# A rehearsal of the final store: the same small store, issued once behind the last weight loads

## The chip, the cores and the metric

One core of one Trainium2 chip. The metric is the device time of one execution in microseconds. The executions of one kernel lie within about 0.5 us of each other here (0.04% of the time). That is larger than the effect studied. So the verdicts below rest on durations inside the traces, which repeat to about 0.02 us. The times are given beside them. The experiments ran on three chips.

Short names used throughout: PE is TensorE, DVE is VectorE, ACT is ScalarE, SP is SyncE. SP issues 78 of the 80 DMAs of the kernel before, ACT the other two.

## The reference, cut to what matters

The whole is a decode step: attention of 2 batch rows over a cache of 32 heads x 16384 positions, mixed by a gate with a small MLP.

```python
x = A_x                                   # (2, 1, 1024) bf16
g = sigmoid((x * gate_w).sum(-1, keepdims=True))
a = attention(x, k_cache, v_cache, wq) @ wo   # caches: 2 x 32 x 16384 x 128 bf16
b = mlp_block(x, w1, w2, w3, w4)
return g * a + (1 - g) * b                # (2, 1, 1024) bf16: 4 KB
```

Two facts matter. The caches and weights are 572 MB to be read once. The output is 4 KB.

## The kernel before: the parts that the change and the argument touch

All work is recorded by a helper, so most instructions have the helper's line, L82. `lane` is the semaphore that the helper has a DMA raise by 16 (`then_inc(lane[0], 16)`), with the value that others wait for; `waits` are further waits. If an operation has several waits, all but the last become wait instructions of their own ahead of it, and the last is carried by the operation itself:

```python
waits = [self.target(o) for o in self.plan[id(op)]] + op.waits
for sem, value in waits[:-1]:
    eng.wait_ge(sem, value)
ins = op.emit()
for sem, value in waits[-1:]:
    ins._wait_ge(sem, value)
```

The start (two small loads on ACT's queue), the end of the loads, and the final store:

```python
R.scalar.dma_start(out=x_rows[0:B, :], in_=A_x..., lane=(row_in[0], 16))
R.scalar.dma_start(out=x_rows[B : B + 1, :], in_=gate_w..., lane=(row_in[1], 16))
# ... weights, 32 K and 32 V loads of the caches on SP, all compute ...
w4 = load_pieces(next_slot(), 0, B_w4, W4_SPLIT, ...)          # 2 pieces
wo = load_pieces(next_slot(), 0, A_wo, WO_SPLIT, ...)          # 7 pieces
R.meet()
# ... the loops over the cache ...
st_down(w4)
wo_stage(wo)
rows = t_tile([P, QW], BF16)
R.vector.tensor_copy(out=rows, in_=out_acc)                     # the cast
R.sync.dma_start(
    out=out.rearrange("b s (g n) -> g (b s) n", g=NQ),          # 4 x 2 rows of 512 B
    in_=rows[0 : P : APART, :],                                 # 8 partitions
    lane=(row_in[0], 32),
)
# ...
nc.sync.wait_ge(row_in[0], 32)
```

`h_rows`, which the change uses as a source, is a tile of the MLP that is written once, at 43.8 us, and read by nobody.

## Time and profile before

| | before |
|---|---|
| time, median of 3 runs | 1329.58 us (1329.5 to 1329.78) |
| span of the profiled execution | 1327.8 us |
| DMA | 572.70 MB, mean 431 GB/s |
| final store: issue on SP / issue to last landing | 0.696 us / 1.740 us |
| end of the cast to SP passing the store's completion ("the stretch") | 1.784 us |

The page of the kernel before: the span, the busy time and share of each engine, and the DMA engines' busy share in 40 equal slices of the span, in tenths.

```profile
span 1327.8 us, 11371 instructions
...
PE 801.6 (60%) x4806; PEld 305.4 (23%) x4859; DVE 762.7 (57%) x1009; ACT 27.2 (2%) x68; POOL 13.2 (1%) x41
...
DMA  9999999999999999999999999999999999999998
```

No compute engine is busy for more than 60% of the span, and the DMA engines are busy at nine tenths or more in every slice but the last. The kernel is bound by its loads until the last byte of weights has landed. What the change can shorten is what follows that moment.

The chain of waits that ended last, over the last 50 us of the kernel before (start, length, what):

```profile
1279.52 44.26 DMA slot<-in_A_wo_dram
1323.78 0.04 issue
1323.83 0.42 PE out_acc L82 x3
1324.24 0.02 issue
1324.27 0.42 DVE T L82
```

The timeline of the tail of the kernel before (start, length, engine, operation), the issues of SP included:

```profile
1276.41 11.12 SPq L82 DMA_DIRECT2D slot<-in_A_wo_dram  x7
...
1323.83 0.39 PE L82 MATMUL out_acc<-slot,T 128*17 128x256 bf16 x4 [0.23 <-DMA slot<-in_A_wo_dram]
1324.27 0.42 DVE L82 CAST T<-out_acc 128x256 bf16<-128x256 f32 x1 [16.30 <-PE out_acc L82]
1324.72 0.70 SPq L82 DMA_DIRECT2D out_dram<-T  x1
```

And of SP's own waits, the one for that store:

```profile
SPq L1027 <- DMA out_dram<-T: 1.0, 1, 1.0
```

Read together: the last piece of `A_wo` lands at 1323.78, four matmuls and the cast take until 1324.69, SP issues the store for 0.70 us and then waits 1.0 us for it to land. About 1.27 us of closing barriers follow. So 4 us of 1327.8 lie behind the loads, and the store is 1.76 us of them.

### The profile page before, as it was taken

Reading aid. Unit: us, or ns where it says so; the run is one execution under the profiler, and the core shown is the slowest. Engines: PE = TensorE matmul, PEld = TensorE weight load, DVE = VectorE, ACT = ScalarE, POOL = GpSimd, SP = SyncE. Lnnn points to the kernel's source line nnn. Section 1 sums busy time; section 2 is a strip of 40 time slices with the busy share of each in tenths; the row PEclk is TensorE's granted clock in tenths of the full one; section 3 lists DMA queues with packets and bytes.
Section 4 is the critical chain, followed back from the end, with each engine's and each line's share of the span. In section 5 each row is a group of like instructions: output and inputs, shape, how many; then the busy total and the mean of one; then the engine's idle time right before and its main releaser. Section 6 shows DMA issues by size and latency. Waiting matters only on the chain. (4 is left out here: it accounts for less than half of the span.)

```text
span 1327.8 us, 11371 instructions
## 1 busy us (share of the span) xinstructions
PE 801.6 (60%) x4806; PEld 305.4 (23%) x4859; DVE 762.7 (57%) x1009; ACT 27.2 (2%) x68; POOL 13.2 (1%) x41
## 2 busy tenths in 40 slices
PE   2767766555566655555765555576655557665553
PEld 1212222122222222222221222222222222222222
DVE  2277676655557665555666555566655556665540
ACT  0000000000000000000000000000000000000000
POOL 0000000000000000000000000000000000000000
PEclk9698887777888877778887777888777788877776
DMA  9999999999999999999999999999999999999998
GB/s 406 443 431 429 433 439 432 434 428 442 432 434 428 442 430 436 428 442 426 438 430 441 426 440 430 440 426 436 434 440 426 436 434 440 426 436 434 440 419 357
DMA packets 11118, 572.70 MB, mean 431 GB/s; under 512 B 1239, under 2 KB 1247, under 8 KB 1634
## 3 DMA queue, kind: packets, MB, share of 16 engines
q1 hardware_dynamic: 11100, 572.53, 99.6%
q8 instruction: 8, 0.13, 0.0%
q14 instruction: 4, 0.03, 0.0%
q10 hardware_dynamic: 6, 0.01, 0.0%
HBM read 572.53 MB, written 0.00 MB: 431 GB/s over the span
## 5 line engine op out<-in xcount | busy, mean ns | idle before, releaser
L526 PE MATMUL S<-T,z 128*128 128x512 bf16 x1933 | 571.6, 426 | 310.7 <-DVE T L517 298.8
L517 DVE STREAM_TRANSPOSE T<-slot 128x1024 f32<-128x1024 f32 x496 | 593.2, 1229 | 247.6 <-DVEq L921 196.0
L526 PEld LDWEIGHTS S<-T,z 128*128 128x128 bf16 x1984 | 171.1, 104 | 698.0 <-DVE T L517 532.5
L577 PE MATMUL O<-slot,PT 128*32 128x512 bf16 x2048 | 119.6, 387 | 7.2 <-PEq L921 7.2
L577 PEld LDWEIGHTS O<-slot,PT 128*32 128x32 bf16 x2048 | 74.0, 140 | 52.2 <-issue 23.0
L588 DVE TENSOR_SCALAR mix<-O,xmask 128x128 f32<-128x128 f32 x32 | 11.2, 351 | 103.6 <-PE O L577 103.6
L543 PE MATMUL tot<-rs,ones_f 128*128 128x2 f32 x62 | 18.2, 363 | 76.4 <-DVE rs L568 76.4
L560 ACT ACTIVATE mix<-S,nb 128x512 bf16<-128x512 f32 x31 | 21.3, 687 | 1158.3 <-DVE nb L550 1158.3
L596 PE MATMUL oc<-asel,mix 128*128 128x2 f32 x64 | 12.3, 262 | 51.8 <-DVE mix L591 51.8
L535 DVE TENSOR_REDUCE m<-S 128x1 f32<-128x512 f32 x31 | 21.4, 691 | 36.3 <-PE S L526 36.3
L565 DVE STREAM_TRANSPOSE PT<-mix 128x512 bf16<-128x512 bf16 x31 | 22.0, 711 | 26.2 <-ACT mix L560 26.2
L591 DVE SCALAR_TENSOR_TENSOR mix<-O,xmask,mix 128x128 f32<-128x128 f32 x96 | 33.7, 351 | 3.4
L543 PEld LDWEIGHTS tot<-rs,ones_f 128*128 128x128 f32 x62 | 15.5, 311 | 82.3 <-DVE rs L568 82.3
L543 PE MATMUL mall<-mix,ones_f 128*128 128x128 f32 x62 | 15.1, 326 | 16.3 <-DVE mix L538 16.3
L596 PEld LDWEIGHTS oc<-asel,mix 128*128 128x128 f32 x64 | 9.5, 188 | 66.2 <-DVE mix L591 66.2
L547 DVE TENSOR_REDUCE mx<-mall 64x1 f32<-64x64 f32 x62 | 13.8, 222 | 18.4 <-PE mall L543 18.0
L82 PE MATMUL out_acc<-slot,T 128*17 128x256 bf16 x240 | 12.1, 361 | 17.1 <-DMA slot<-in_A_wo_dram 9.3
L508 POOL TENSOR_TENSOR z<-qsel,own 128x32 bf16<-128x32 bf16 x31 | 10.5, 340 | 1167.3 <-PE O L577 1167.3
L82 PE MATMUL S<-T,z 128*128 128x512 bf16 x62 | 17.9, 416 | 6.3 <-DVE T L82 5.9
L82 DVE STREAM_TRANSPOSE T<-slot 128x1024 f32<-128x1024 f32 x16 | 19.1, 1228 | 1.6 <-PE S L82 1.3
L573 DVE RECIPROCAL rinv<-tot 128x2 f32<-128x2 f32 x31 | 5.3, 170 | 21.1 <-PE tot L543 21.1
L599 DVE TENSOR_TENSOR OT<-oc,rinv 128x2 f32 x32 | 5.1, 159 | 15.2 <-PE oc L596 15.2
(115 smaller groups left out, 129.5 us busy)
## 6 DMA issues: line engine op xcount, KB each, us to landing
slot<-in_B_w_dram SPq DMA_DIRECT2D x1, 7168.0 KB, 48.5
slot<-in_B_w_dram SPq DMA_DIRECT2D x2, 3584.0 KB, 28.4
slot<-in_A_wo_dram SPq DMA_DIRECT2D x3, 2048.0 KB, 37.2
slot<-in_B_w_dram SPq DMA_DIRECT2D x2, 2048.0 KB, 29.2
slot<-in_A_wo_dram SPq DMA_DIRECT2D x1, 1024.0 KB, 43.5
slot<-in_A_k_cache_dram SPq DMA_DIRECT2D x32, 49.3
slot<-in_A_v_cache_dram SPq DMA_DIRECT2D x32, 35.1
slot<-in_A_wo_dram SPq DMA_DIRECT2D x1, 512.0 KB, 44.3
```

The costliest lines, as they stand in the source:

```text
L82: op = Op(engine, lambda: getattr(eng, method)(*args, **kwargs), reads, writes, waits, lane)
L517: return vector.transpose(out=t_tile([P, 2, CJ, 32], FP32, m % 2).rearrange("p w j s -> p j w s"), in_=K[:].bitcast(FP32)[:, m * CW : (m + ...
L526: return tensor.matmul(S, lhsT=z[:, v, NM - 1 - m : NM - 1 - m + P], rhs=Tb[:, v // 2, :, v % 2], start=(m == 0 and v == 0), stop=(m == NM ...
L535: return vector.reduce_max(out=stat["m"][:], in_=S, axis=AX.X)
L543: return tensor.matmul(ps, lhsT=ones_f[:], rhs=src, start=True, stop=True)
L547: return vector.reduce_max(out=stat["mx"][pa, :], in_=mall[pa, pa], axis=AX.X)
L560: return scalar.activation(out=Pr, in_=S, func=ACTF.Exp, bias=stat["nb"][:], scale=scale, accum_out=stat["rs"][:])
L565: return vector.transpose(out=PT[:], in_=Pr)
L577: return tensor.matmul(O[32 * g : 32 * g + 32, :], lhsT=PT[:, m : CJ * 32 : 16], rhs=V[:].rearrange("p (j d) -> p j d", d=Dh)[:, j0 : j0 + ...
L588: return vector.tensor_scalar(out=Os, in0=Ox, scalar1=xmask[:, 0:1], scalar2=None, op0=ALU.mult)
L591: return vector.scalar_tensor_tensor(out=Os, in0=Ox, scalar=xmask[:, x : x + 1], in1=Os, op0=ALU.mult, op1=ALU.add)
L596: return tensor.matmul(oc, lhsT=Os, rhs=asel[:], start=True, stop=True)
```

## The change: its intent, and the diff

The idea is to pay in advance what the first store of this form may cost. A store of the same shape (the same rows of the output, 8 source partitions of 512 B; only the step between the source partitions differs, 8 in place of 16) is issued behind the last weight loads, while SP has nothing to do (in the kernel before, its last load issue ends at 1287.53 us and its next issue begins at 1324.72). The final store overwrites what it writes, so it must come second. The order of issue on SP alone can't be relied on for that: with a rehearsal of one row (below), the rehearsal landed at 1322.26 us and the piece of `A_wo` issued before it at 1323.77. So the final store now waits for the first one too. Without the wait, that would be a race.

```diff
         [(sem["free"], 2 * LAST + 2)],
     )
+    out_rows = out.rearrange("b s (g n) -> g (b s) n", g=NQ)
+    R.sync.dma_start(out=out_rows, in_=h_rows[0:64:8, 0:QW], lane=(row_in[1], 32))
     R.meet()
 ...
     R.sync.dma_start(
-        out=out.rearrange("b s (g n) -> g (b s) n", g=NQ),
-        in_=rows[0 : P : APART, :],
+        out=out_rows,
+        in_=rows[0:P:APART, :],
         lane=(row_in[0], 32),
+        waits=[(row_in[1], 32)],
     )
```

The final store now has two waits, so by the code shown above the wait for the cast becomes an instruction of its own, and the store carries the wait for the rehearsal.

## The prediction

> What bounds the kernel now. The page shows DMA busy at nine tenths or more in 39 of 40 slices and 431 GB/s over the span of 1327.8 us (572.53 MB read): the load queue is the limit, PE (60%) and DVE (57%) are not. The change touches only the tail, read from the timeline of the last 60 us, the chain of waits, and the trace's packet and semaphore records:
>
> - SP issues the seven pieces of A_wo from 1276.41. The seventh is held in the queue for 8.0 us (1279.52 to 1287.53) until the last V load has landed (1287.27).
> - The last 2 KB packets end at 1323.47, the last piece lands at 1323.78, PE finishes at 1324.24, the DVE cast runs 1324.27 to 1324.69.
> - The final store is issued at 1324.72; its issue takes 0.70 us on SP; its 512-byte packets run 1326.02 to 1326.12; SP passes its completion wait at 1326.48. Issue to landing is 1.76 us; 1.27 us of closing barriers follow.
>
> What the change adds. One more 4 KB store in the same queue, of rows that are overwritten (8 packets of 512 B, some 25 ns each). SP should reach it at about 1287.6; as the seventh A_wo piece had to wait for an older load, I expect the new issue to be held too, until the first B_w4 piece lands (about 1295.7). SP is free until 1324.7, so this costs nothing. Its packets stand behind the last A_wo piece[...]. They should run by 1323.6 at the latest and land some 0.35 us later (as the final store's did), about 1323.9: 0.8 us before the final store is ready. The new wait should be met. The second wait costs the final store one more sequencer instruction, 0.04 to 0.08 us (gaps between SP's instructions in the tail).
>
> What it may save. The final store is the first of its form on SP. Its issue takes 696 ns, while A_wo and cache loads take 327 to 432. On the ACT queue the first small load took 542 ns and the second, of a slightly different form, 234 ns. If a first use of a form costs extra, a rehearsal some 30 us earlier removes 0.2 to 0.5 us of the 1.76 us, all on the critical path. But the form itself may cost it[...]: one early update at 1325.79, then four at 1326.40 to 1326.46. Such a cost stays. Estimate: save 0.35, pay 0.06, net -0.3 us.
>
> Predicted: 1329.3 us, 80% range 1328.7 to 1329.9. Faster by over 2%: 0.2%; within 2%: 99.6%; slower by over 2%: 0.2%.
>
> What would show it. Right: a second store of 4 KB in the table of issues; the last A_wo landing, PE and cast unmoved within 0.1 us; the final store's issue shorter than 0.70 us, and issue to landing 1.3 to 1.6 us. Wrong in the saving: its issue again near 0.70 us and landing again 1.76 us after; then the time is 1329.6 to 1329.7.
>
> What would make it wrong. The rehearsal lands later than 1324.7, so the final store waits for it: up to 1 us slower. Or another chip moves all by more than the effect.

The rehearsal delays no load (measured: the last load landed 0.05 us later, within the spread between runs).

## The result, and the profile after

The time is 1329.52 us (median of 6 runs, 1329.42 to 1329.69), against 1329.61 us for the kernel before in 6 runs (1329.36 to 1329.78). The ratio is 0.9999, with a 95% interval of 0.9987 to 1.0012. A ratio is the mean time of one kernel's fast runs over that of the other's in the same rounds, so it is not quite the ratio of the medians quoted. By the times alone the two kernels are the same.

The same lines of the page after the change:

```profile
span 1327.7 us, 11373 instructions
...
PE 800.0 (60%) x4806; PEld 304.5 (23%) x4859; DVE 763.1 (57%) x1009; ACT 27.2 (2%) x68; POOL 13.1 (1%) x41
...
DMA  9999999999999999999999999999999999999998
```

The chain of waits after the change, over the same stretch:

```profile
1279.32 44.51 DMA slot<-in_A_wo_dram
1323.83 0.04 issue
1323.87 0.42 PE out_acc L82 x4
1324.29 0.02 issue
1324.32 0.42 DVE T L82
```

SP's issues at the end, after the change, and below them SP's waits for the cast and for the final store:

```profile
1279.32 8.29 SPq L82 DMA_DIRECT2D slot<-in_A_wo_dram  x1
1287.66 7.20 SPq L82 DMA_DIRECT2D out_dram<-h_rows  x1
1324.84 0.54 SPq L82 DMA_DIRECT2D out_dram<-T  x1
```

```profile
SPq L162 <- DVE T L82: 29.9, 1, 29.9
...
SPq L1030 <- DMA out_dram<-T: 1.1, 1, 1.1
```

The loads, the matmuls and the cast are where they were: the last load lands 0.05 us later, which is noise (over all runs it lands between 1323.64 and 1324.04). The rehearsal's issue blocks SP for 7.20 us, at a time when SP has nothing else to do. The wait for the cast now stands at a line of its own, L162, ahead of the store. The final store starts later behind the cast, and its issue is shorter: 0.54 us in place of 0.70.

The trace's instruction, packet and semaphore records give the tail more finely (us from the span's start):

| | before | after |
|---|---|---|
| rehearsal landed | - | 1323.814 |
| last load landed | 1323.781 | 1323.828 |
| cast ends | 1324.692 | 1324.742 |
| final store's issue begins | 1324.719 | 1324.838 |
| its issue takes | 0.696 | 0.538 |
| end of the issue to first semaphore update (the early one; see below) | 0.377 | 0.418 |
| first data packet begins | 1326.016 | 1326.022 |
| last landing | 1326.459 | 1326.454 |
| SP passes the wait | 1326.476 | 1326.469 |
| **issue to last landing** | **1.740** | **1.616** |
| **cast's end to SP passing ("stretch")** | **1.784** | **1.727** |

The early update is one that comes before any data packet of the store: at 1325.792 before the change, 0.22 us ahead of the first packet. Four more follow the data (1326.401 to 1326.459). The last piece of `A_wo` ends in 16 updates and has no early one; ACT's two small loads at the start have an early one each (1.585 and 1.943 us), then two and one. The records do not name the DMA engines. Where a DMA is said below to run on four of them, on two, on one, on few or over 16, this is the reading of these counts of updates behind the data.

So the books read: the issue is 0.158 us shorter; 0.041 of this is given back before the first update; issue to landing gains 0.124 us; the extra wait instruction takes 0.069 of it (the gap from cast to issue grew from 0.027 to 0.096). In all the tail is 0.057 us shorter. The mean times differ by 0.07 us in the same direction, but that alone would prove nothing.

### The profile page after: what moved, and what is told of

It reads as the page before. It is cut to its first block, busy times and chain, and to the rows that moved or that the text cites. A ratio compares the mean times of both kernels' runs of the same rounds, so it can differ in the third digit from the quotient of the medians.

```text
span 1327.7 us, 11373 instructions
## 1 busy us (share of the span) xinstructions
PE 800.0 (60%) x4806; PEld 304.5 (23%) x4859; DVE 763.1 (57%) x1009; ACT 27.2 (2%) x68; POOL 13.1 (1%) x41
```

## The experiments

Twelve kernels ran, two of them twice, all with correct results. Theory A: the first DMA of a form on a queue costs extra, and the rehearsal pays it in advance. Rival B: nothing was rehearsed; the issue only looks shorter because a separate wait instruction now goes ahead of it, so that the store no longer sits waiting for the cast itself. Two numbers judge them: the final store's issue time, and the stretch. The table has them all, and the runs follow one by one.

| run | issue, ns | issue to landing, us | stretch, us | time, median (runs), us | before in the same rounds, us |
|---|---|---|---|---|---|
| before | 696 | 1.740 | 1.784 | 1329.61 (6) | - |
| after | 538 | 1.616 | 1.727 | 1329.52 (6) | 1329.61 |
| wait alone | 699 | 1.745 | 1.857 | 1329.58 (4) | 1329.55 |
| waits swapped | 538 | 1.616 | 1.662 | 1329.36 (4) | 1329.55 |
| rehearsal is a load | 587 | 1.665 | 1.774 | 1329.41 (4) | 1329.55 |
| rehearsal at 49 us | 567 | 1.648 | 1.761 | 1329.70 (4) | 1329.55 |
| two rehearsals | 527 | 1.617 | 1.731 | 1329.52 (4) | 1329.63 |
| rehearsal at 1319 us | 538 | 1.629 | 1.743 | 1329.58 (4) | 1329.63 |
| store from ACT, none | 644 | 1.734 | 1.782 | 1329.68 (4) | 1329.63 |
| rehearsal of one row | 665 | 1.748 | 1.862 | 1329.57 (4) | 1329.63 |
| ACT's loads swapped, none | 696 | 1.759 | 1.802 | 1329.69 (1) | 1329.59 |
| met wait on rehearsal | 537 | 1.615 | 1.728 | 1329.74 (1) | 1329.59 |
| after, again | 537 | 1.631 | 1.744 | 1329.46 (5) | 1329.59 |
| waits swapped, again | 538 | 1.620 | 1.665 | 1329.52 (5) | 1329.59 |

No time in the table stands clear of the spread; the columns to its left do.

### The wait alone, without the rehearsal

```diff
-    R.sync.dma_start(out=out_rows, in_=h_rows[0:64:8, 0:QW], lane=(row_in[1], 32))
 ...
-        waits=[(row_in[1], 32)],
+        waits=[(row_in[1], 16)],     # met since the start of the kernel
```

> No rehearsal; the final store has a second wait, on a count that was reached at the start, so SP runs the same two instructions as after the change (a wait for the cast, then the store). Measured in the trace: the store's issue on SP (before 696 ns, after 538 ns) and the stretch from the end of the cast to SP passing the store's completion (before 1.78 us, after 1.73 us). First-use theory: issue near 696 ns, stretch near 1.85 us (the extra instruction's 0.07 us is paid, nothing is saved), time about 1329.7. Rival, that the issue is shorter only because a separate wait instruction goes ahead of it: issue near 538 ns, stretch near 1.73 us, time about 1329.5.

Its SP line at the tail:

```profile
1325.03 0.70 SPq L82 DMA_DIRECT2D out_dram<-T  x1
```

The issue takes 699 ns with a wait instruction ahead of it, and the stretch grows to 1.857 us: 0.07 us over the kernel before. Rival B fails: the wait by itself only costs. The price of 0.07 us for one more wait instruction on the critical path is confirmed.

### The two waits in the other order

```diff
+            if getattr(op, "own_first", False):
+                waits = op.waits + [self.target(o) for o in self.plan[id(op)]]
 ...
-    R.sync.dma_start(
+    final = R.sync.dma_start(
 ...
+    final.own_first = True
```

> Rehearsal kept; the two waits of the final store change places, so that the separate wait instruction is the one on the rehearsal (met about 0.9 us early) and the store itself waits for the cast, as before the change. First-use theory: issue near 538 ns and the extra 0.07 us gone from the stretch: about 1.65 us, time about 1329.4. Rival (the separate instruction shortens the issue): issue back near 696 ns, stretch near 1.78 us, time about 1329.6.

SP's waits and its issues, with the waits in the other order:

```profile
SPq L164 <- DMA out_dram<-h_rows: 28.9, 1, 28.9
```

```profile
1287.54 7.32 SPq L82 DMA_DIRECT2D out_dram<-h_rows  x1
1324.64 0.54 SPq L82 DMA_DIRECT2D out_dram<-T  x1
```

The separate instruction is now the wait for the rehearsal, which is met at 1323.82, 0.8 us before the store may go. The store carries the wait for the cast, as in the kernel before, and its issue still takes 538 ns: theory A again, against B. The 0.07 us are gone and the stretch is 1.662 us. This is the best tail, 0.12 us under the kernel before.

### A load of the same split as the rehearsal

```diff
-    R.sync.dma_start(out=out_rows, in_=h_rows[0:64:8, 0:QW], lane=(row_in[1], 32))
+    R.sync.dma_start(
+        out=h_rows[0:64:8, 0:QW],
+        in_=B_x.rearrange("b s (g n) -> g (b s) n", g=NQ),
+        lane=(row_in[1], 32),
+    )
```

> The rehearsal is a load of the same split (4 x 2 rows of 512 B[...]), from the input B_x into the same rows that the store would have read; all else as after the change. If what the first use costs belongs to the split over few engines: final issue near 538 ns, as after the change. If it belongs to a store, or to the output tensor: near 696 ns and a stretch near 1.85 us.

```profile
1287.48 7.28 SPq L82 DMA_DIRECT2D h_rows<-in_B_x_dram  x1
1324.64 0.59 SPq L82 DMA_DIRECT2D out_dram<-T  x1
```

The line above is SP's issue of the load, the line below it the final store: 587 ns. A load that does not touch the output pays 109 of the 158 ns. So most of the first-use price belongs to what the load shares with the store: eight rows of 512 B in the same 4 x 2 split. The other 49 ns need a store, or this exact pattern, or this tensor; the run doesn't tell which.

The run also answers a rival that has not been named: that the final store is faster only because it stands at another place in SP's stream of instructions. The trace records 82 SP instructions ahead of the final store here, in the changed kernel and in the run with a rehearsal of one row below; the issue takes 587, 538 and 665 ns.

### The rehearsal 1275 us earlier

```diff
     load_k(1)
+    out_rows = out.rearrange("b s (g n) -> g (b s) n", g=NQ)
+    R.sync.dma_start(out=out_rows, in_=h_rows[0:64:8, 0:QW], lane=(row_in[1], 32))
 ...                                    # and taken out behind the last loads
```

> The rehearsal store is moved from the end of the loads to behind the second cache load, about 49 us into the span, 1275 us and some 65 loads before the final store. Its own issue is not held by the queue there: first-use theory says near 700 ns for it. If the gain lasts: final issue near 538 ns, stretch near 1.73 us. If other loads in between undo it: near 696 ns, stretch near 1.85 us. Rival (wait instruction): its own issue, without a separate wait ahead or with one, says nothing; final issue 538 ns in either case.

SP's issues near 49 us of that run, then its final store:

```profile
48.64 0.33 SPq L82 DMA_DIRECT2D slot<-in_A_k_cache_dram  x1
49.01 0.70 SPq L82 DMA_DIRECT2D out_dram<-h_rows  x1
```

```profile
1325.03 0.57 SPq L82 DMA_DIRECT2D out_dram<-T  x1
```

Here the rehearsal is not held, and its own issue shows the first-use price openly: 703 ns, as the final store's 696 without a rehearsal. The final store, 71 loads later, still takes only 567 ns. Most of what was paid is kept over 1275 us; 29 ns of it are lost. As the queue had no small DMA near the final store here, a queue that was used shortly before is not what shortens the issue.

### Two rehearsals

```diff
     load_k(1)
+    # the early rehearsal, lane=(row_in[1], 32)
 ...
+    R.sync.dma_start(out=out_rows, in_=h_rows[0:64:8, 0:QW],
+                     lane=(row_in[1], 48), waits=[(row_in[1], 32)])
 ...
+        waits=[(row_in[1], 48)],      # of the final store
```

> Two rehearsal stores: one at 49 us, as in the run with the early rehearsal, and one behind the last loads, as after the change. The final store is then the third of its form on SP. If all that a first use costs is paid once and for all, the final issue stays at 538 ns (what is left is the form's own cost); if each use makes the next cheaper, it is well under 538 ns, 450 or less. Stretch from the end of the cast to SP passing the store's completion near 1.73 us in the first case.

SP's last issues in that run:

```profile
1287.58 0.57 SPq L82 DMA_DIRECT2D out_dram<-h_rows  x1
1324.79 0.53 SPq L82 DMA_DIRECT2D out_dram<-T  x1
```

Three stores of one form take 703, 568 and 527 ns. The last step is small and gives nothing at the landing (1.617 us from issue, against 1.616). So about 530 ns are what this form costs after two earlier uses; no rehearsal tried here goes below that. A side result: the second rehearsal was not held (0.57 us), though it stands where the one of the change was held for 7.2 us. See the met wait below.

### The rehearsal late, 6 us before the final store

```diff
-    R.sync.dma_start(out=out_rows, in_=h_rows[0:64:8, 0:QW], lane=(row_in[1], 32))
+    R.sync.dma_start(out=out_rows, in_=h_rows[0:64:8, 0:QW], lane=(row_in[1], 32),
+                     waits=[(v_in[1], 16)])     # the third piece of A_wo
```

> The rehearsal waits until the third piece of A_wo has landed (about 1318.9), so it is issued some 6 us before the final store and is not held by the queue: its own issue should take 700 ns, the first-use price with no hold. It still lands by 1323.9, behind the last loads. If the gain depends on how lately the form was used (567 ns after 1275 us, 538 ns after 30 us): final issue at or a little under 538 ns. If 538 is the form's own floor: 538 ns again, stretch 1.73 us.

```profile
1318.82 0.69 SPq L82 DMA_DIRECT2D out_dram<-h_rows  x1
1324.79 0.54 SPq L82 DMA_DIRECT2D out_dram<-T  x1
```

These are SP's two stores in that run. The first takes the first-use price (687 ns), the second 538 ns, the same as with a rehearsal 37 us ahead. Nearness gains nothing more. The rehearsal landed at 1323.91, in time though it was issued only 5 us earlier.

### The final store from ACT's queue

```diff
-    R.sync.dma_start(
+    R.scalar.dma_start(
         out=out.rearrange("b s (g n) -> g (b s) n", g=NQ),
```

> The kernel before, with its final store issued from ACT, whose queue has had two small loads on few DMA engines at the start (542 and 234 ns). No rehearsal and no second wait. If what a rehearsal pays in advance is paid by any DMA on few engines and is kept per issuing engine (a load of this split gave 587 ns, an early store 567 ns): issue about 560 to 620 ns and stretch about 1.68 us, as good as the rehearsal without its extra wait. If ACT's long run of other instructions undoes it: near 700 ns, stretch near 1.78 us.

```profile
1324.86 0.64 ACTq L82 DMA_DIRECT2D out_dram<-T  x1
```

The issue takes 644 ns on ACT, and the stretch is 1.782 us: nothing gained. No run shows what this store takes on ACT without the two small loads at the start (on two engines and on one), so 644 ns can't be set against SP's 696. What the run shows is that they don't serve as a full rehearsal: 644 is far above 538. Whether they never did, or 1320 us of other instructions undid it, stays open.

### A rehearsal of one row

```diff
-    R.sync.dma_start(out=out_rows, in_=h_rows[0:64:8, 0:QW], lane=(row_in[1], 32))
+    R.sync.dma_start(out=h_rows[0:1, :],
+                     in_=gate_w.rearrange("(o d) -> o d", o=1)[:, 0:HW],
+                     lane=(row_in[1], 32))
```

> The rehearsal is a load of one row of 1 KB[...], into a row of the same tile that nothing reads. If any DMA on fewer than 16 engines pays the first-use price: final issue near 587 ns, as with the load of the same split. If the split over four engines or the several rows matter: between 590 and 700 ns; near 700 ns if nothing of it is shared.

```profile
1287.51 5.82 SPq L82 DMA_DIRECT2D h_rows<-in_gate_w_dram  x1
1324.78 0.67 SPq L82 DMA_DIRECT2D out_dram<-T  x1
```

The final issue (second line, SP) takes 665 ns, and issue to landing is 1.748 us, not shorter than without any rehearsal: the 31 ns that the issue saves come back before the first semaphore update (0.411 us after the issue's end, against 0.377). So being a small DMA is not enough. (The kernel before loads a row of `gate_w` too, and that load has one update behind its data, where a piece of `A_wo` has 16.) What the load of eight rows paid belongs to its several rows, or perhaps to several engines that they run on; these runs do not tell the two apart.

### ACT's two first loads in the other order

This run tests the evidence on which the prediction sized the gain: on ACT the first small load took 542 ns and the second 234 ns.

```diff
-        R.scalar.dma_start(out=x_rows[0:B, :], in_=A_x..., lane=(row_in[0], 16))
         R.scalar.dma_start(out=x_rows[B : B + 1, :], in_=gate_w..., lane=(row_in[1], 16))
+        R.scalar.dma_start(out=x_rows[0:B, :], in_=A_x..., lane=(row_in[0], 16))
```

> The kernel before, with the two small loads that ACT issues at the start in the other order: first the one row of gate_w[...], then the two rows of A_x[...]. Before, the first took 542 ns and the second 234 ns, which the prediction took for a first use and a second. If the 308 ns between them are mostly a first-use price: gate_w, now first, takes 450 ns or more and A_x, now second, 300 ns or less. If they are the forms' own: gate_w near 234 ns to 350 ns and A_x near 400 to 542 ns.

ACT's issues at the start of the kernel before:

```profile
0.96 0.54 ACTq L82 DMA_DIRECT2D T<-in_A_x_dram  x1
...
1.54 0.23 ACTq L82 DMA_DIRECT2D T<-in_gate_w_dram  x1
```

And with the two loads in the other order:

```profile
0.96 0.52 ACTq L82 DMA_DIRECT2D T<-in_gate_w_dram  x1
...
1.51 0.25 ACTq L82 DMA_DIRECT2D T<-in_A_x_dram  x1
```

Whichever goes first takes 516 to 542 ns, and the second 234 to 247 ns. So the 0.27 to 0.31 us go with being first and not with the form: on ACT they are a first-use price. What exactly was used for the first time is not shown. It may be the engine's first DMA of all, or its first on few DMA engines; on ACT they are the same one. SP's own first DMA shows no such price: its first load took 397 ns and its second 407. Nor does SP's first load of the caches: 328 ns, and 327 to 328 for the later ones.

### The changed kernel with a met wait on the rehearsal

```diff
-    R.sync.dma_start(out=out_rows, in_=h_rows[0:64:8, 0:QW], lane=(row_in[1], 32))
+    R.sync.dma_start(out=out_rows, in_=h_rows[0:64:8, 0:QW], lane=(row_in[1], 32),
+                     waits=[(row_in[1], 16)])
```

> After the change, and the rehearsal carries a wait that was met at the start of the kernel. Its issue took 7.2 us after the change but 568 ns in the run with two rehearsals, where it carried such a wait and an earlier store had gone ahead. If the wait makes the difference: about 700 ns. If the earlier store did[...]: 7.2 us again. The final store: issue 538 ns and stretch 1.73 us either way.

```profile
1287.84 7.44 SPq L82 DMA_DIRECT2D out_dram<-h_rows  x1
1325.05 0.54 SPq L82 DMA_DIRECT2D out_dram<-T  x1
```

SP's rehearsal is held for 7.44 us again. So the wait that it carries is not why the second of two rehearsals went through in 0.57 us. What an earlier store changes there stays open. It costs nothing, as SP has nothing to do before 1324.5 in any version with a rehearsal there.

### The changed kernel, and the swapped waits, once more

> The changed kernel again, as a measure of how well the trace's numbers repeat: final issue 538 ns, issue to landing 1.62 us, stretch 1.73 us, each within 0.02 us; time 0.05 us under the kernel before, which five rounds (spread of single runs about 0.4 us) can't show with certainty.

> The kernel with the rehearsal and the waits of the final store in the other order, again: final issue 538 ns, stretch 1.66 us; time 0.12 us under the kernel before and 0.07 us under the changed kernel, at the edge of what the mean of five rounds shows.

The final store's issue in the two runs:

```profile
1324.75 0.54 SPq L82 DMA_DIRECT2D out_dram<-T  x1
```

```profile
1324.94 0.54 SPq L82 DMA_DIRECT2D out_dram<-T  x1
```

The traces repeat: issue 537 and 538 ns, stretches 1.744 and 1.665 us (first time 1.727 and 1.662). The run with ACT's loads swapped, on the same chip, has the tail of the kernel before: 696 ns and 1.802 us. So on this chip the change gains 0.058 us in the tail, and 0.137 us with the waits swapped. The times do not separate the versions. The mean of five runs is 1329.51 us for the changed kernel and 1329.49 us with the waits swapped, against 1329.59 us before; the ratios are both 0.9999, with intervals of 0.9986 to 1.0013 and 0.9985 to 1.0013. The moment at which the last load lands moves more from run to run (0.40 us between the extremes) than all that the store can gain.

## Why the prediction was right or wrong, point by point

- **"The load queue is the limit" and the change touches only the tail: right.** Over the last 50 us the chain takes the same steps before and after, and its last load lands 0.05 us later, well within the 0.40 us by which this moment moves from run to run.
- **The rehearsal is free where it stands: right.** It was held for 7.20 us in place of the 8.1 predicted (1287.6 to 1295.7), SP being idle; it landed at 1323.81, predicted 1323.9, 0.9 us before the cast was done. The reason given for the hold was wrong: it ended 0.9 us before the first `B_w4` piece had landed (1295.78), in the run with the rehearsal of one row (held until 1293.33) before any part of that piece had (1293.96), and in one version there was no hold. What ends it stays open. For the hold of the seventh `A_wo` piece, from which this was inferred, the traces do agree: in all 14 it ended 0.26 to 0.28 us after the last V load had landed.
- **The second wait costs one more instruction, 0.04 to 0.08 us: right,** 0.069 us here, and 0.07 us when it was all that was changed.
- **A first use of the form costs extra and the rehearsal takes it away: right in kind.** The run with the wait alone (699 ns), the swapped waits (538 ns) and the early rehearsal's own issue (703 ns) show it, and rule out rival B.
- **"Removes 0.2 to 0.5 us of the 1.76 us", estimate 0.35: this is the step that was wrong.** It measured 0.124 us from issue to landing. Three things made the term too large. First, the size was borrowed from ACT's first and second load. That difference is real on ACT, as the swap shows, but it is one between ACT's first DMA of the kernel and its second. SP had issued 77 loads before its final store (1 `A_wq`, 5 `B_w`, 64 cache loads, 7 `A_wo`), and there a first use of this form cost 158 ns. That those loads had paid the rest is a guess; SP's first load (397 ns) shows no such price. Second, the comparison with the 327 to 432 ns of loads over 16 engines took a difference of form for a difference of first and later use; the third store of the form still takes 527 ns. Third, 0.04 us of the shorter issue came back between the end of the issue and the first semaphore update (0.377 or 0.378 us on SP without a rehearsal, 0.416 to 0.418 us in all versions that rehearse this store, 0.411 and 0.415 us where a load was the rehearsal).
- **The sum.** Predicted -0.35 + 0.06, about -0.3 us; measured in the trace -0.124 + 0.069, about -0.06 us. The time, 1329.52 us, lies inside the predicted range and "within 2%" holds, but so would no effect at all: the kernel before, 1329.61 us, lies inside it too. The time is therefore no evidence for the mechanism; the issue times are. "Issue to landing 1.3 to 1.6 us" missed slightly: 1.63 us by the prediction's own measure, to SP's passing.

What is not settled is what SP does in the 158 ns. The price is paid once, mostly kept for 1275 us (567 ns, against 696 without a rehearsal) and partly shared with a load of the same split (587 ns). No record in these traces shows what is done in that time.

The prediction allowed that the form itself may cost a part of the issue, and pointed to the store's updates: one early at 1325.79, then four from 1326.40 to 1326.46. No rehearsal here removes these: all 14 traces show the early update and the four. What makes the early one, and whether it costs SP time, is not shown. How much of the 527 to 538 ns it makes up was not measured.

The DMAs of SP did not all land in the order of issue: the rehearsal, issued behind the last piece of `A_wo`, had three of its four updates by 1322.60 and the last at 1323.814, and the piece of `A_wo` ended at 1323.828. In the run with the rehearsal of one row the difference is plain: the rehearsal landed at 1322.26, the piece issued before it at 1323.77.

## What to carry to other kernels

A first use can have a price, and it differs from place to place: here 0.27 to 0.31 us for ACT's first DMA, 0.16 us for SP's first store of this form, and none for SP's first load of the caches (328 ns, the later ones 327 to 328). Before you borrow the size of such an effect from another place in the trace, ask what is used there for the first time, and whether the same is still unused where you want the gain.

When an instruction gets a second wait, let the one that is met early be the separate instruction, and let the instruction itself carry the wait that ends last: here that order alone was worth 0.07 us, more than the rest of the change had kept. And where runs scatter by more than the effect, measure the stretch between two events inside the trace, and repeat it.

## What else the traces measured

- First-use price of a DMA issue: the first DMA that ACT issued took 516 to 557 ns in the 14 traces and the second 234 to 247 ns, in either order; the first store of this form on SP took 687 to 703 ns with no small DMA ahead of it, 527 to 568 ns after an earlier store of the form, and 587 ns after a load of the same split.
- The early semaphore update of the store: before the change it came 0.22 us before the first data packet began, so it did not wait for the store's data. For this store it came 0.94 to 1.08 us after the issue began, 0.38 to 0.42 us after it ended.
- Where the time of this small store goes, issued from SP: before the change, 1.30 of 1.74 us passed before the first packet began (0.60 us of it after SP's issue had ended; 0.65 us after the change), and 0.36 us from the start of the last 512-byte packet to the last landing.
- An issue was held for long with SP blocked: before the change the seventh piece of `A_wo` was held for 8.0 us (in all 14 traces until 0.26 to 0.28 us after the last V load had landed), and after it the rehearsal behind that piece for 7.2 us.
